# A windowed attention with a two-layer network behind it: early transposes on TensorE, a shorter weight conversion with a second reading, other due times

## The chip, the cores and the metric

The kernel runs on one NeuronCore of one Trainium2 chip. TensorE (PE) multiplies matrices into PSUM, which has eight banks; VectorE (DVE), ScalarE (ACT) and GpSimd (POOL) work on tiles of 128 partitions; SyncE (SP) issues nearly all DMAs, in program order. Each engine works through its own list of instructions in order and waits at semaphores. The metric is the device time of one execution in microseconds, the median of three runs.

## The reference

Attention with a local window and a few global columns, for 4 batches and 8 heads of 768 rows and 64 columns; then a layer of 512 to 2048, a sigmoid gate, and 2048 to 512, on all 3072 rows:

```python
scores = scale * np.matmul(q, k.transpose(0, 1, 3, 2)) + bias      # scale = 1 / sqrt(64)
scores = np.where(is_global | is_local, scores, -1e9)              # n_global = 8, n_local = 96
a = np.exp(scores - np.max(scores, axis=-1, keepdims=True))
a = a / (np.sum(a, axis=-1, keepdims=True) + 1e-09)
x = np.matmul(a, v)            # to (3072, 512)
h = x @ w_in                   # w_in (512, 2048)
g = h * (1.0 / (1.0 + np.exp(-1.702 * h)))
out = g @ w_out                # w_out (2048, 512)
```

q, k and v are float32, the weights float64 (read as pairs of 32-bit words).

## The kernel before

**Attention.** The 3072 rows are 24 blocks of 128 (`n` 0 to 23), six to a batch. A block's rows look at their own block, the one before, and the batch's first 32 columns, so a unit (two of the eight heads, `u` 0 to 3) has score tiles of 128 or 256 columns. `prep` loads a block's q, k and v (three DMAs of 256 KB), splits them into a high and a low float16 (L338 to L348), transposes both by DMA into `QK` (L341) and copies its halves across (the swap, L343). A `unit` is then a chain: scores on TensorE (L377) into the single PSUM buffer `s`; on VectorE mask and row minimum (L383, tile `p` and `NM`); the exponential on ScalarE (L392); a float16 copy (L396) and the remainder (L398) into `hl`; a DMA transpose of both into `pt` (L399); values on TensorE (L408 to L410) into `pv`. `leading` copies the batch's first columns and rows over the block's own when the block is done with its own (L427; L429 is a DMA, `VR<-VG`, that waits for the last values of the block). `finish` divides by the row sum, splits, and transposes by DMA into `xT` (L456).

**Network.** Two blocks make a chunk `c` (0 to 11). The 2048 inner columns are eight slices `s`. `up` multiplies (24 matmuls, L473, tile `h`), then the gate runs: tanh on ScalarE (L482), VectorE (L483), ScalarE (L484), VectorE (L485, tile `g`). `down` adds into `y` (12 matmuls, L500). After slice 7 `y` is scaled and written out (L511, L513). Every product is three float16 products (high by high, high by low, low by high).

**Weights.** For each slice the up half (`u` = 0) and the down half (`u` = 1) are loaded as 1 MiB of word pairs (`ws`, L159). Four passes move the float64's exponent and mantissa into float32 `wa` and two split it into `w`, high and low (L287 to L296). They stay in SBUF. Later ScalarE sums their squares once (L558), for a check; blocks 0 to 3 are loaded once more for theirs (tile `again`). If a check fails, `general` computes everything anew in a slower way; its instructions stand behind a branch.

**What sets the order.** Every step is a task with the engines it may run on, a cost in us, its buffers and a due time. Due times are pulled back from a task's followers, and `order` then plays the queues: on a free engine the ready task with the earliest due time is taken, if its buffers are free and it is due within `AHEAD` = 25 us. The instructions of each engine stand in the order that comes out. Slices of chunks 0 and 1 take turns while weights arrive (`seq`, `PACE0`), later chunks follow one by one (`PACE`). In the tables and rows a tile's name carries block and unit, chunk and slice, or slice and half: `pt2_3` is block 2, unit 3; `h1_0` chunk 1, slice 0; `w3_1` slice 3, down half.

## Time and profile before

| | us |
|---|---|
| median of three runs (lowest to highest) | 664.21 (663.39 to 668.5) |
| the profiled execution, its time | 665.1 |
| its span, first to last instruction | 663.3 |
| TensorE busy | 588.8 |
| ScalarE busy | 427.4 |
| VectorE busy | 412.4 |
| GpSimd busy | 11.6 |

The mean granted clock of TensorE is 0.985. The profile cuts the span into 40 slices of 16.6 us; a digit is the busy share of a slice in tenths:

```profile
PE   0134959999899999999999999999999999999995
DVE  5788789888656557556555655665656645554321
ACT  3677879987557567646656758888755666552321
```

A row of a table of groups reads: line, engine, operation, output <- input, shapes, count | busy us, mean ns of one | idle us of the engine just ahead of them <- what ended it. In rows of stretches each engine's busy us and number of instructions follow the length; PEclk is the granted clock, then the DMA engines' mean busy share (transfers overlap, so it may pass 1) and GB/s. In lists of waits stand total us, times and the longest.

### The profile page before, as it was taken

To read this page: it belongs to the slowest core of one execution; us is meant where nothing else is said; L and a number is where in the kernel's file an instruction comes from. 1 tells how busy PE (TensorE), PEld (TensorE's weight loads), DVE (VectorE), ACT (ScalarE), POOL (GpSimd) and SP (SyncE) were. 2 spreads that over 40 slices of the span, in tenths; PEclk is the share of its full clock that TensorE was granted. 3 is DMA by queue.
4 is the path that set the end of the run, shared out by engine and by line. 5 is a ranking of instruction groups with operands and counts; after the bars stand their busy time and mean duration, and the time that the engine had idled before them with its cause. 6 is when DMAs were issued, how large, how long until landed. Compare 5 with 4: busy or idle time off the path is not lost.

```text
span 663.3 us, 13356 instructions
## 1 busy us (share of the span) xinstructions
PE 588.8 (89%) x5218; PEld 418.1 (63%) x5218; DVE 412.4 (62%) x969; ACT 427.4 (64%) x925; POOL 11.6 (2%) x14
## 2 busy tenths in 40 slices
PE   0134959999899999999999999999999999999995
PEld 0123737677477777677666677776676776776762
DVE  5788789888656557556555655665656645554321
ACT  3677879987557567646656758888755666552321
POOL 1500000000000000000000000000000000000000
PEclk9999989999899999999999999999999999999998
DMA  9999999746968569649619838659819684432001
GB/s 192 243 206 255 243 276 313 205 86 137 227 136 151 125 113 177 136 87 175 152 37 164 158 76 173 137 106 184 186 38 165 143 179 101 95 63 54 33 1 38
DMA packets 270824, 95.61 MB, mean 144 GB/s; under 512 B 257824, under 2 KB 257824, under 8 KB 270752
## 3 DMA queue, kind: packets, MB, share of 16 engines
q1 hardware_dynamic: 270464, 94.66, 67.4%
q8 instruction: 43, 0.70, 0.5%
q14 instruction: 29, 0.24, 0.1%
q10 hardware_dynamic: 288, 0.00, 0.0%
HBM read 38.80 MB, written 6.29 MB: 68 GB/s over the span
## 4 chain that ended last, share of the span: by engine, by line
PE 84%; DMA 7%; DVE 4%; issue 2%; SPq 1%; ACT 1%; DVEq 0%; ACTq 0%
PE h L473 38%; PE y L500 36%; PE s L377 6%; PE pv L408 2%; PE pv L410 2%; PE pv L409 1%; DMA ws<-in_moe_w_in_dram 1%; DMA pt<-hl 1%; DMA QK<-qk 1%; DVE p L383 1%; DMA QK<-QK 1%; DMA VR<-VG 1%; DMA raw<-in_k_dram 1%; DVE qk L339 1%; SPq L341 1%
## 5 line engine op out<-in xcount | busy, mean ns | idle before, releaser
L473 PE MATMUL h<-xT,w 128*128 128x256 f16 x2304 | 269.0, 275 | 3.7 <-DMA xT<-x 3.4
L500 PE MATMUL y<-w,g 128*128 128x512 f16 x1152 | 264.9, 381 | 0.0
L473 PEld LDWEIGHTS <-w 128*128 128x128 f16 x2304 | 223.7, 99 | 33.3 <-issue 4.1
L500 PEld LDWEIGHTS <-g 128*128 128x128 f16 x1152 | 110.1, 98 | 116.8 <-issue 1.9
L392 ACT ACTIVATE p<-p,NM 128x256 f32<-128x256 f32 (+1 forms) x192 | 92.2, 481 | 40.1 <-DVE NM L383 39.4
L482 ACT ACTIVATE t<-h 128x512 f32<-128x512 f32 x96 | 57.0, 593 | 80.5 <-PE h L473 80.0
L383 DVE CUSTOM_DVE_ANT_0 p<-s,mm 128x256 f32<-128x256 f32 (+1 forms) x192 | 69.7, 398 | 61.9 <-PE s L377 61.6
L483 DVE SCALAR_TENSOR_TENSOR t<-t,h 128x512 f32<-128x512 f32 x96 | 65.6, 683 | 61.2 <-ACT t L482 61.1
L377 PE MATMUL s<-QK 128*128 128x128 f16 x384 | 51.4, 234 | 42.4 <-DMA QK<-QK 18.4
L377 PEld LDWEIGHTS <-QK 128*128 128x128 f16 x704 | 48.9, 104 | 63.4 <-DMA QK<-QK 19.1
L485 DVE SCALAR_TENSOR_TENSOR g<-t,g 128x512 f16<-128x512 f32 x96 | 66.1, 688 | 29.4 <-ACT g L484 29.2
L484 ACT ACTIVATE g<-t 128x512 f16<-128x512 f32 x96 | 60.0, 625 | 29.3 <-DVE t L483 28.4
L398 DVE TENSOR_TENSOR hl<-p,hl 128x512 f16<-128x512 f32 (+1 forms) x96 | 61.4, 643 | 23.8 <-ACT hl L396 23.6
L396 ACT CAST hl<-p 128x512 f16<-128x512 f32 (+1 forms) x96 | 55.7, 581 | 6.3 <-DMA pt<-hl 3.8
L408 PE MATMUL pv<-VR,pt 128*128 128x64 f16 x352 | 42.1, 198 | 12.6 <-DMA pt<-hl 8.6
L377 PE MATMUL s<-QK,QK 128*128 128x128 f16 x320 | 43.2, 231 | 7.8 <-DVE NM L383 7.8
L408 PEld LDWEIGHTS <-pt 128*128 128x128 f16 x352 | 33.9, 101 | 18.8 <-DMA pt<-hl 9.6
L410 PE MATMUL pv<-VR,pt 128*128 128x64 f16 x352 | 42.2, 198 | 0.0
L409 PE MATMUL pv<-VR,pt 128*128 128x64 f16 x352 | 42.2, 198 | 0.0
L409 PEld LDWEIGHTS <-pt 128*128 128x128 f16 x352 | 33.1, 101 | 4.5
L392 ACT ACTIVATION_READ_ACCUMULATOR p<-p,NM 128x1 f32 x192 | 36.0, 187 | 0.0
L339 DVE SCALAR_TENSOR_TENSOR qk<-raw,qk 128x1024 f16<-128x1024 f32 x24 | 29.6, 1234 | 9.6 <-ACT qk L338 9.4
(80 smaller groups left out, 392.2 us busy)
## 6 DMA issues: line engine op xcount, KB each, us to landing
ws<-in_moe_w_in_dram SPq DMA_DIRECT2D x8, 1024.0 KB, 6.3
ws<-in_moe_w_out_dram SPq DMA_DIRECT2D x8, 1024.0 KB, 7.6
raw<-in_q_dram SPq DMA_DIRECT2D x24, 256.0 KB, 3.4
raw<-in_k_dram SPq DMA_DIRECT2D x24, 256.0 KB, 3.8
raw<-in_v_dram SPq DMA_DIRECT2D x24, 256.0 KB, 3.6
QK<-QK SPq DMA_DIRECT2D x48, 128.0 KB, 3.4
out_dram<-yo SPq DMA_DIRECT2D x24, 256.0 KB, 2.5
pt<-hl SPq DMA_TRANSPOSE x96, 3.3
```

The costliest lines, as they stand in the source:

```text
L377: nc.tensor.matmul(sp()[:, j, s * P:(s + 1) * P], d["QK"]()[:, 0, h, :], K[:, 1 + z, h, :], start=(z == 0), stop=(z == 1), skip_group_chec ...
L383: nc.vector.tensor_tensor_reduce(out=pr()[:, j, :], in0=sp()[:, j, :], in1=m, scale=-1.0 / SC, scalar=3.0e38, op0=ALU.add, op1=ALU.min, ac ...
L392: ex.append(add({"ACT": 0.48 + 0.1 * ns}, lambda e, j=j: nc.scalar.activation(pr()[:, j, :], pr()[:, j, :], AF.Exp, bias=NM[:, n, hs[j]:hs ...
L398: lambda e: ENG[e].tensor_sub(hl()[:, 1], pr(), hl()[:, 0]), [t4], [pr, hl])
L408: nc.tensor.matmul(o, ph, V[:, 0, h], start=(s == 0), stop=False, skip_group_check=True)
L409: nc.tensor.matmul(o, ph, V[:, 1, h], start=False, stop=False, skip_group_check=True)
L473: nc.tensor.matmul(ph()[:, fi, :], w1(s, cc, z, fi), X[:, y, cc, :], start=(j + cc == 0), stop=(j == 2 and cc == NCC - 1))
L482: t2 = add({"ACT": 0.62}, lambda e: nc.scalar.activation(t(), hh(), AF.Tanh, scale=0.851 / (SX * SW)), [t1], [ph, t])
L483: t3 = add({"DVE": 0.7}, lambda e: nc.vector.scalar_tensor_tensor(t(), t(), 1.0, hh(), ALU.add, ALU.mult), [t2], [ph, t])
L484: t4 = add({"ACT": 0.62}, lambda e: nc.scalar.mul(g()[:, 0], t(), SG / (SX * SW)), [t3], [t, g])
L485: t5 = add({"DVE": 0.7}, lambda e: nc.vector.scalar_tensor_tensor(g()[:, 1], t(), SG / (SX * SW), g()[:, 0], ALU.mult, ALU.subtract), [t4] ...
L500: nc.tensor.matmul(y()[:, t], G[:, zg, fi, t * P:(t + 1) * P], w2(s, z, fi), start=(s == 0 and j == 0 and fi == 0), stop=(s == NST - 1 and ...
```

## The change

Four parts.

1. For blocks 0 to 3 (`EARLY`) TensorE transposes the exponentials themselves, in float32 against an identity matrix, into a PSUM tile `tp`; ScalarE casts them from there into the high half of `pt` and VectorE writes the remainder. `hl` and the DMA transpose drop out for these blocks: 8 transposes for block 0 and 16 each for blocks 1 to 3. The PSUM tiles are borrowed from `y`, which becomes four rings of one bank.
2. In the weights' conversion ScalarE writes the sign as bfloat16 1 or -1 into the upper half of each word of the addend, in place of VectorE's sign mask, and the pass that scaled the exponent (L287) drops out; VectorE shifts `ws` directly. The last two steps now also scale.
3. That holds only for weights in a range of exponents, so all weights are loaded a second time: ScalarE sums the squares of the high words, VectorE takes their minimum, and the end tests both.
4. Due times: attention of chunk 2 and later 60 in place of 46 us ahead of its chunk, `PACE0` 8.0 and `PACE` 5.9, and the checks start from fixed earliest times. Rings: `hl` 3 to 2, `pt` 5 to 4.

```diff
-        t1 = add({"ACT": 1.05}, lambda e: nc.scalar.mul(wa(), ws()[:, :, 1].bitcast(F32), 2.0 ** -111), [t0], [ws, wa])
-        t2 = add({"DVE": 0.7}, lambda e: nc.vector.tensor_scalar(ai(), ai(), 3, None, ALU.logical_shift_left), [t1], [wa])
-        t3 = add({"DVE": 0.75}, lambda e: nc.vector.tensor_scalar(
-            part(1), ws().bitcast(U16)[:, :, 3::4].rearrange("p c o -> p (c o)"), 1 << 15, None, ALU.bitwise_and), [t0], [ws, w])
-        t4 = add({"ACT": 1.05}, lambda e: nc.scalar.mul(part(0), ws()[:, :, 0].bitcast(U32), 2.0 ** -29), [t0], [ws, w])
+        t2 = add({"DVE": 0.75}, lambda e: nc.vector.tensor_scalar(ai(), ws()[:, :, 1], 3, None, ALU.logical_shift_left),
+                 [t0], [ws, wa])
+        t3 = add({"ACT": 1.35}, lambda e: nc.scalar.activation(part(1).bitcast(BF16), ws()[:, :, 1].bitcast(F32), AF.Sign), [t0], [ws, w])
+        t4 = add({"ACT": 1.35}, lambda e: nc.scalar.mul(part(0), ws()[:, :, 0].bitcast(U32), 2.0 ** -29), [t0], [ws, w])
         t5 = add({"DVE": 1.25}, lambda e: nc.vector.tensor_add(ai(), ai(), extra()), [t2, t3, t4], [w, wa])
-        t6 = add({"ACT": 1.05}, lambda e: nc.scalar.copy(w()[:, 0], wa()), [t5], [wa, w])
-        t7 = add({"DVE": 1.25}, lambda e: nc.vector.tensor_sub(w()[:, 1], wa(), w()[:, 0]), [t6], [wa, w])
+        t6 = add({"ACT": 1.05}, lambda e: nc.scalar.mul(w()[:, 0], wa(), 2.0 * SW), [t5], [wa, w])
+        t7 = add({"DVE": 1.25}, lambda e: nc.vector.scalar_tensor_tensor(
+            w()[:, 1], wa(), 2.0 * SW, w()[:, 0], ALU.mult, ALU.subtract), [t6], [wa, w])
...
+        if n < EARLY:
+            tp = Buf(r_y[1, u % 2] if n > 1 else r_y[u // 2, u % 2], [P, 2 * ns, P], F32, f"tp{n}_{u}")
+            def turn(e):
+                for j in range(2):
+                    for s in range(ns):
+                        nc.tensor.transpose(tp()[:, j * ns + s, :], pr()[:, j, s * P:(s + 1) * P], ident)
+            t4 = add({"PE": 2 * ns * 0.215}, turn, ex, [pr, tp])
+            t5 = add({"ACT": 0.2 + 0.21 * ns}, lambda e: nc.scalar.copy(pt()[:, 0:2 * ns], tp()), [t4], [tp, pt])
+            t6 = add({"DVE": 0.15 + 0.27 * ns}, lambda e: nc.vector.tensor_sub(pt()[:, 2 * ns:4 * ns], tp(), pt()[:, 0:2 * ns]),
+                     [t5], [tp, pt])
+        else:
...
-    T0, PACE0, PACE = 25.0, 6.5, 6.05
+    T0, PACE0, PACE = 25.0, 8.0, 5.9
...
-                ws_ = start[c, 0] - 46.0 + 5.2 * ((n % 2) * NU + u)
+                ws_ = start[c, 0] - 60.0 + 5.2 * ((n % 2) * NU + u)
...
+            ws = Buf(r_ws, [P, 1024, 2], I32, f"ws{s}_{u}again")
+            t0 = add({"SP": 3.2}, lambda e, s=s, u=u, ws=ws: load_weights(nc, ws(), w_in, w_out, s, u), bufs=[ws])
+            soon, hi_w = 190.0 + 20.0 * (2 * s + u), lambda ws=ws: ws()[:, :, 1].bitcast(F32)
+            t1 = add({"ACT": 1.35}, lambda e, s=s, u=u, hi_w=hi_w: nc.scalar.activation(
+                hi_w(), hi_w(), AF.Square, accum_out=e2[:, 0, 2 * s + u:2 * s + u + 1]), [t0], [ws])
+            add({"DVE": 1.3}, lambda e, s=s, u=u, hi_w=hi_w: nc.vector.tensor_reduce(
+                e2[:, 1, 2 * s + u:2 * s + u + 1], hi_w(), axis=AX.X, op=ALU.min), [t1], [ws])
+            t0.soon = soon
```

How the order moves, at three places. First SP's queue from the transpose that completes `xT0` on. Before:

```order
L456 DMA_TRANSPOSE xT0_464<-x161_535 128x8x128
L159 DMA ws3_0_558<-in_moe_w_in_dram 128x4x512
L399 DMA_TRANSPOSE pt2_3_617<-hl2_3_556 128x8x128
L159 DMA ws3_1_634<-in_moe_w_out_dram 128x2x1024
L399 DMA_TRANSPOSE pt3_0_707<-hl3_0_615 128x8x128
L399 DMA_TRANSPOSE pt3_1_717<-hl3_1_666 128x8x128
L159 DMA ws4_0_736<-in_moe_w_in_dram 128x4x512
L429 DMA VR2_318<-VG0_238 32x1024
L399 DMA_TRANSPOSE pt3_2_781<-hl3_2_763 128x8x128
L456 DMA_TRANSPOSE xT1_800<-x162_775 128x8x128
L399 DMA_TRANSPOSE pt3_3_808<-hl3_3_779 128x8x128
L159 DMA ws4_1_813<-in_moe_w_out_dram 128x2x1024
```

The same stretch after the change, up to the transpose that completes `xT1`:

```order
L476 DMA_TRANSPOSE xT0_366<-x161_517 128x8x128
L449 DMA VR2_176<-VG0_161 32x1024
L319 DMA raw4_497<-in_v_dram 128x8x64
L164 DMA ws3_0_766<-in_moe_w_in_dram 128x4x512
L164 DMA ws3_1_788<-in_moe_w_out_dram 128x2x1024
L476 DMA_TRANSPOSE xT1_857<-x162_784 128x8x128
L319 DMA raw5_864<-in_q_dram 128x8x64
L319 DMA raw5_864<-in_k_dram 128x8x64
L449 DMA VR3_309<-VG0_161 32x1024
L164 DMA ws4_0_920<-in_moe_w_in_dram 128x4x512
L476 DMA_TRANSPOSE xT1_857<-x163_918 128x8x128
```

The transposes of `pt` are gone, and the copy into `VR2`, which stood behind the weights of slice 4, now stands ahead of those of slice 3.

Second, ScalarE between the first gate's end and the third, where the down half of slice 2 gets its cast. Before:

```order
L484 ACTIVATE g0_0_769<-t0_0_709 128x512
L482 ACTIVATE t0_1_771<-h0_1_682 128x512
L293 ACTIVATE w3_0_720<-ws3_0_558 128x1024
L396 CAST hl3_3_779<-p3_3_711 128x512
L293 ACTIVATE w3_1_784<-ws3_1_634 128x1024
L482 ACTIVATE t0_2_803<-h0_2_738 128x512
L484 ACTIVATE g0_1_806<-t0_1_771 128x512
L295 CAST w3_0_720<-wa3_0_714 128x1024
L293 ACTIVATE w4_0_840<-ws4_0_736 128x1024
L295 CAST w2_1_541<-wa2_1_621 128x1024
L484 ACTIVATE g0_2_857<-t0_2_803 128x512
```

After, from the second gate's tanh on:

```order
L504 ACTIVATE g0_1_862<-t0_1_794 128x512
L301 ACTIVATE w2_1_809<-ws2_1_394 128x1024
L502 ACTIVATE t0_2_894<-h0_2_829 128x512
L300 ACTIVATE w3_0_912<-ws3_0_766 128x1024
L301 ACTIVATE w3_0_912<-ws3_0_766 128x1024
L300 ACTIVATE w3_1_924<-ws3_1_788 128x1024
L301 ACTIVATE w3_1_924<-ws3_1_788 128x1024
L303 ACTIVATE w2_1_809<-wa2_1_915 128x1024
L504 ACTIVATE g0_2_935<-t0_2_894 128x512
```

The cast of `w2_1` stood behind conversions of slices 3 and 4; it now stands behind the sign and the low word (L300, L301) of both halves of slice 3.

Third, TensorE at the start of batch 1's attention (block 6). Before:

```order
L377 MATMUL s6_0_1900<-QK6_1801 128x128
L377 LDWEIGHTS QK6_1801
L377 MATMUL s6_0_1900<-QK6_1801 128x128
L377 LDWEIGHTS QK6_1801
L377 MATMUL s6_1_1916<-QK6_1801 128x128
L377 LDWEIGHTS QK6_1801
L377 MATMUL s6_1_1916<-QK6_1801 128x128
```

After:

```order
L385 MATMUL s6_0_1894<-QK6_1764 128x128
L385 LDWEIGHTS QK6_1764
L385 MATMUL s6_0_1894<-QK6_1764 128x128
L520 LDWEIGHTS g1_6_1846
L520 MATMUL y1_0_1071<-w6_1_1252,g1_6_1846 128x512
L520 LDWEIGHTS g1_6_1846
L520 MATMUL y1_0_1071<-w6_1_1252,g1_6_1846 128x512
```

Unit 1's scores directly followed unit 0's; now a whole down of chunk 1 stands between them. The same holds for the other blocks.

More of the change, by code (lines that the diff above doesn't have):

```diff
@@ L26 @@
 LOW = 1e8
+EARLY = 4
 AHEAD = 25.0
@@ L61, in __init__, with early @@
         self.on, self.fn, self.after, self.bufs, self.due = on, fn, list(after), list(bufs), want
-        self.next, self.end, self.eng, self.start = [], None, None, None
+        self.next, self.end, self.eng, self.start, self.soon = [], None, None, None, 0.0
+    def early(self):
+        return self.soon if self.due > 1e8 else self.due - AHEAD
 class Work:
@@ L107, in order @@
                 for t, at in ready.items():
-                    if e not in t.on or at > now or t.due > now + AHEAD or (best is not None and t.due >= best.due):
+                    if e not in t.on or at > now or t.early() > now or (best is not None and t.due >= best.due):
                         continue
@@ L146, in order @@
             if not moved:
-                later = [t.due - AHEAD + 1e-6 for t in ready if t.due > now + AHEAD]
+                later = [x + 1e-6 for x in (t.early() for t in ready) if x > now]
                 later += [x for x in (*free.values(), dma - BACKLOG + 1e-6) if x > now] + [at for at in ready.values() if at > now]
@@ L216 @@
     nc.vector.tensor_add(odd, odd, o2)
+    ident = const.tile([P, P], F32, name="ident")
+    make_identity(nc, ident)
     mm = const.tile([P, H, 3, P], BF16, name="mm")
@@ L252 @@
     swt = const.tile([P, 2, NST], F32, name="swt")
+    e2 = const.tile([P, 2, 2 * NST], F32, name="e2")
     junk = const.tile([P, 1024], BF16, name="junk")
@@ L265 @@
     r_s, r_pv = ring("s", 1, ps), ring("pv", 1, ps)
-    r_h, r_y = ring("h", 2, ps), ring("y", 2, ps)
+    r_h = ring("h", 2, ps)
+    r_y = {(z, t): ring(f"y{z}{t}", 1, ps) for z in range(2) for t in range(2)}
     r_w = {(s, u): ring(f"w{s}_{u}", 1) for s in range(NST) for u in range(2)}
@@ L490, in down @@
         if s == 0:
-            ys[c] = Buf(r_y, [P, 2, DM], F32, f"y{c}")
+            ys[c] = [Buf(r_y[c % 2, t], [P, DM], F32, f"y{c}_{t}") for t in range(2)]
         y = ys[c]
@@ L510, in down @@
                 t2 = add({"DVE": 0.7, "ACT": 0.65}, lambda e, t=t, yo=yo: (
[L511 to L512 removed]
+                    nc.vector.tensor_scalar(yo(), y[t](), f, None, ALU.mult) if e == "DVE" else nc.scalar.mul(yo(), y[t](), f)),
+                    [t1], [y[t], yo], want + 4)
                 add({"SP": 0.7}, lambda e, t=t, yo=yo: nc.sync.dma_start(
@@ L554 @@
         raw = Buf(r_raw, [P, 3, H, D], F32, f"again{n}")
-        guard(n, raw, load(n, raw), t_ - 150.0 + 20 * n)
+        ld = load(n, raw)
+        guard(n, raw, ld, 1e9)
+        for t in ld:
+            t.soon = 400.0 + 30 * n
     for s in range(NST):
```

28 lines of the change are left out of this document (14 added, 14 removed).

## The prediction

> **What bounds the kernel now.** I read the busy shares first, then one table of stages cut where the chain of waits turns.
>
> ```profile
> PE 588.8 (89%) x5218; PEld 418.1 (63%) x5218; DVE 412.4 (62%) x969; ACT 427.4 (64%) x925; POOL 11.6 (2%) x14
> ```
>
> ```profile
> core 0: us, PE busy (x) PEld busy (x) DVE busy (x) ACT busy (x) POOL busy (x), PEclk, DMA share, GB/s
> 0.00:33.00 33.00, 3.02 (x19) 1.92 (x19) 21.21 (x64) 16.15 (x31) 11.62 (x14) 1.00 0.97 217
> 33.00:66.00 33.00, 12.67 (x138) 10.40 (x139) 27.62 (x66) 25.39 (x54) 0.00 (x0) 1.00 1.17 230
> 66.00:98.10 32.10, 23.81 (x233) 16.84 (x232) 26.31 (x53) 25.21 (x43) 0.00 (x0) 0.94 1.10 256
> 98.10:178.30 80.20, 77.30 (x644) 54.13 (x644) 68.95 (x133) 65.97 (x126) 0.00 (x0) 0.97 0.76 197
> 178.30:655.20 476.90, 471.86 (x4188) 334.77 (x4186) 266.84 (x647) 294.08 (x675) 0.00 (x0) 0.99 0.59 118
> 655.20:663.30 8.10, 0.17 (x3) 0.06 (x2) 1.48 (x9) 0.60 (x1) 0.00 (x0) 0.65 0.21 76
> ```
>
> There are two regimes. From 98.1 us to 655.2 TensorE is the bound: it works 549.2 of 557.1 us. Before 98.1 it works only 39.5 us, while the DMA share stands at or above 1: there the transfers are the bound. The chain of waits says what they hold up, and the list of PE's waits after 100 us what is left later:
>
> ```profile
> 71.01 2.62 PE h L473 x24
> ...
> 80.54 5.59 DMA VR<-VG
> ...
> 94.70 3.40 DMA xT<-x
> ...
> 98.14 9.55 PE h L473 x72
> ...
> 655.25 0.14 PE pb L583 x2
> ```
>
> ```profile
> PE s L377 <- DVE NM L383: 7.6, 7, 1.7
> PE h L473 <- DVE t L483: 0.2, 1, 0.2
> ```
>
> So the time is the start T of h1_0 (chunk 1's first up-projection, 98.14 now), plus 557.1 us of nearly gapless TensorE, plus a tail of 8.05 us. In both orders the same TensorE work stands ahead of h1_0: attention of blocks 0 to 3, three ups, three downs. That makes T a fair mark.
>
> **Step 1, transposes off the DMA queue.** Sixteen transposes (blocks 0 to 3) leave SP's queue.
>
> ```profile
> L399 SPq DMA_TRANSPOSE pt<-hl x16: 1214/1376/4092, 30.2 to 85.8; - x16
> ...
> DMA to landing us min/median/max: 2.5/5.8/9.9
> ```
>
> I count bytes from the rows of the order and the tiles' shapes. Up to the transpose that completes xT0 (it frees h0_0) the old queue moves 14.75 MiB: 3 of raw, 6 of weights, 2 of QK, 1 of swaps, 2.25 of pt, 0.5 of xT. The new one moves 13.0: no pt, but 0.5 of raw4 pulled forward. With the transfers as the bound, h0_0 comes at 71.01 x 13.0 / 14.75 = 62.6. Up to the transpose that completes xT1 it is 21.5 against 17.25 MiB, so transfers alone would allow T = 98.14 x 17.25 / 21.5 = 78.7. That is the lower end.
>
> **The wait that takes its place.** The new queue puts VR2<-VG0 (the copy of the leading rows into block 2's values) ahead of raw4's v, both halves of weights 3, both transposes of xT1 and weights 4_0. The copy waits for the last values matmul of block 2, which TensorE's order now puts behind h0_0 and h0_1. That this copy waits for TensorE is old:
>
> ```profile
> SPq L429 <- PE pv L410: 32.1, 6, 9.3
> ```
>
> From h0_0 at 62.6 to that matmul TensorE has two ups, two score units, two groups of four transposes and three of values. Its clock decides how long:
>
> ```profile
> 38.28 0.42 PE L377 MATMUL s<-QK 128*128 128x128 f16 x2
> 38.49 0.42 PE L377 MATMUL s<-QK,QK 128*128 128x128 f16 x2
> ...
> 86.97 4.44 PE L500 MATMUL y<-w,g 128*128 128x512 f16 x12
> ...
> 91.95 2.75 PE L500 MATMUL y<-w,g 128*128 128x512 f16 x12
> ```
>
> Two 128-column matmuls start 0.21 us before the next two, 0.107 each: half speed, since the dense stretch does twelve of 512 columns in 2.75 us and the one after the wait at 80.54 needed 4.44. I take the first up at about 4.3 (2.62 x 4.44 / 2.75), the second at 2.6, and 4.3 for the small groups: 11.2, so the copy is issued near 73.8. Then 4.25 MiB (4.46 MB) follow; at the 256 GB/s of the 66 to 98.1 row that is 17.4 us, and some 2 us until the first lands: xT1 is whole near 93.2. ScalarE gives the same time: it takes the third down's weight cast (w2_1) only behind both halves of weights 3, which land near 85; two conversions, the cast, g's two steps and the down end near 93. **T = 93**, 5.1 earlier. Between the ends 78.7 and 98.1 I take a value near the upper one because of this wait, and because of ScalarE's share: it has done 66.8 us by 98.1, 78% of the time from 33 on. Counted by the order with the durations of the rows, the new one leaves it 2.2 less by h1_0's tanh; T = 93 asks for 77%, T = 78.7 for 100%, T = 86 for 87%.
>
> **What TensorE gets.** 56 f32 transposes of 128 columns; none is in the trace. Lower end 0.107 each (6 us), upper four such passes (24 us). Most run before 62, in the 58.6 idle us ahead of 98.1; 20 run behind h0_0 and lie in the 4.3 and in T. I take 0.2. The Trainium skill, "TensorE: Matmul & The Clock Gate", section on the PE-mode transpose, gives about 275 ns in a kernel, by which the 56 would be 15.4 us, and says that transposes do not count as activity for the clock; no trace here shows it. The eviction's two steps keep their sizes (casts and subtractions of the same shapes):
>
> ```profile
> L396 ACT CAST hl<-p 128x512 f16<-128x512 f32 x80 | 49.2, 617 | 5.6 <-DMA pt<-hl 3.5
> L398 DVE TENSOR_TENSOR hl<-p,hl 128x512 f16<-128x512 f32 x80 | 54.8, 687 | 23.0 <-ACT hl L396 22.9
> ```
>
> **Step 2, the weights' exponents.** A tile costs ScalarE 1.144 + 1.354 + 1.040 and VectorE 0.765 + 0.686 + 1.228 + 1.234 now.
>
> ```profile
> L293 ACT ACTIVATE w<-ws 128x1024 uint16<-128x1024 uint32 x16 | 21.7, 1354 | 2.4 <-DMA ws<-in_moe_w_out_dram 2.4
> L296 DVE TENSOR_TENSOR w<-wa,w 128x1024 f16<-128x1024 f32 x16 | 19.6, 1234 | 0.3 <-ACT w L295 0.3
> L294 DVE CUSTOM_DVE_ANT_0 wa<-wa,w 128x2048 uint16<-128x2048 uint16 x16 | 19.5, 1228 | 1.2 <-ACT w L293 0.8 <-issue 0.2
> L287 ACT ACTIVATE wa<-ws 128x1024 f32<-128x1024 f32 x16 | 18.2, 1144 | 13.1 <-DMA ws<-in_moe_w_in_dram 7.6 <-DMA ws<-in_moe_w_out_dram 5.5
> L295 ACT CAST w<-wa 128x1024 f16<-128x1024 f32 x16 | 16.5, 1040 | 2.3 <-DVE wa L294 2.3
> L291 DVE TENSOR_SCALAR w<-ws 128x1024 uint16<-128x1024 uint16 x16 | 12.2, 765 | 6.0 <-DMA ws<-in_moe_w_out_dram 3.1 <-DMA ws<-in_moe_w_in_dram 2.9
> L288 DVE TENSOR_SCALAR wa<-wa 128x1024 int32<-128x1024 int32 x16 | 10.9, 686 | 1.3 <-ACT wa L287 1.2
> ```
>
> Afterwards the sign (written every second 16-bit word, as L293 does) costs 1.144 to 1.354, I take the latter: ScalarE +0.21, +3.4 in all. VectorE loses one pass, about -0.70 a tile, -11.2 in all. A tile's first VectorE step no longer waits for ScalarE. This lies in the early stage, inside T; it earns nothing by itself where the queue is late.
>
> **Step 3, the second reading.** 16 MiB more, 16.8 MB. At the rate of a stretch full of weights it takes 53.6 us of the queue, spread between about 190 and 500 us, where the DMA share of 0.59 has room (16.8 MB over 477 us raises it by about 0.11). ScalarE gets 16 squares with a sum (1.144 + 0.19), VectorE 16 minima:
>
> ```profile
> 99.50:116.10 16.60, 16.60 (x123) 12.17 (x122) 15.98 (x22) 15.80 (x23) 0.00 (x0) 0.95 1.04 313
> ```
>
> ```profile
> L318 ACT ACTIVATION_READ_ACCUMULATOR junk<-raw 128x1 f32 x40 | 7.6, 190 | 0.0
> L569 DVE TENSOR_REDUCE fin<-NM 128x1 f32<-128x192 f32 x1 | 0.3, 346 | 0.0
> ```
>
> The minimum, 1024 elements, lies between 0.346 and 5.3 times that; I take about 1.2. ScalarE +21, VectorE +19 beside 294 and 267 of 477: covered, as long as no square holds up an exp behind it while its load is still on the way. I allow 3 us for such waits, from 0 to rival 3's price.
>
> **Step 4, attention sooner.** All seven of PE's late waits are at places where two score units stand directly behind each other; the single `s` buffer makes the second wait for VectorE. In the new order something else of TensorE's stands between any two units from block 0's third on. That removes the 7.8 us of the two rows. What is late next: nothing in the row, TensorE itself. Around the first such place it also loses its clock:
>
> ```profile
> 174.00:181.00 7.00, 4.14 (x28) 2.99 (x26) 3.65 (x20) 6.89 (x24) 0.00 (x0) 0.67 1.03 243
> ```
>
> 0.33 of 7 us, 2.3 us, goes with the waits. At nothing I cost the separate y banks and the shorter rings (hl 3 to 2, pt 5 to 4), since the list of late waits names neither y nor pt and the units now come 14 us sooner; the identity matrix on POOL, which works 11.6 of the first 33 us; four small VectorE steps more ahead of the last sum, done under TensorE's last three downs; and block 0's scores, which come some us earlier (their swap now precedes weights 0_1) but are followed by block 1's, whose swap still stands behind weights 1_0.
>
> **Sum.** 93 + (557.1 - 7.8 - 2.3 + 3) + 8.05 = 651.05. The profiled run took 665.1 for a span of 663.3 (+1.8) and lies 0.9 over the median of 664.21, so 652.
>
> **Rivals.** 1. The earlier start is given back: ScalarE (65.97 of 80.2 us between 98.1 and 178.3) cannot take the later half of the weights faster, h2_0 starts at 178.3 as now, and only the 5.0 idle us behind it go: 658.3, as a time 659. For it: VectorE and ScalarE at 82% or more there; against: VectorE loses 11 us. 2. The queue does not wait so long (h0_0 warm, the copy early), T = 86, with 0 to 3 us of new waits: 642 to 645. For it: transfers alone allow 78.7. 3. Slower: the squares wait for their loads.
>
> ```profile
> ws<-in_moe_w_out_dram SPq DMA_DIRECT2D x8, 1024.0 KB, 7.6
> ```
>
> ScalarE keeps its order, so a square ahead of its data holds exps, tanhs and at last TensorE. At 2 us each, 652 - 3 + 32 = 681; it decides from 1.4 us each (671), and 7.6 would be the whole landing. Against it: they are issued in a stage with slack. 4. The clock stays at half through blocks 2 and 3, because transposes do not wake it: three ups and three downs of 2.6 at nearly double, some 11 us on T after the queue's cover: 663, no change. Against it: h0_0 alone is 24 ordinary matmuls, and now the clock rises within the first such groups. The rule of the Trainium skill's "TensorE: Matmul & The Clock Gate" named above would lead here. 5. The new check refuses these weights, and the general path recomputes everything: more than double the time.
>
> **Chances.** Forecast (T 89 to 97; 648 to 657) 0.56; rival 1 0.19; rival 2 0.14; rival 3 0.06; rival 4 0.04; rival 5 0.01. A measurement here tells about 1%, 657.6 to 670.9 being no change. Faster: 0.56 + 0.14 = 0.70; same: 0.19 + 0.04 = 0.23; slower 0.07. The range takes in most of rivals 1 and 2: 642 to 661.
>
> **What would show it.** h0_0 near 63; VR2<-VG0 issued near 74 with SP waiting on values matmuls and the DMA share dipping under 1 ahead of it; h1_0 near 93; no wait of PE on NM after 100; ScalarE waiting little on the second weights. It is wrong if h1_0 starts before 86 or after 98, if PE idles over 8 us between h1_0 and the end, or if transposes take over 0.43 us each.

## The result and the profile after

The changed kernel takes 646.18 us (median of four runs, 644.56 to 647.04) against 666.36 us for the kernel before in the same session (663.39 to 670.38): a ratio of 0.969, 95% interval 0.963 to 0.975. It is faster, by 20 us; the prediction said 652. The profiled execution took 644.56 us, the shortest of the four, for a span of 642.8.

First the busy shares and the table of stages, cut at the same events as before (the fourth row starts shortly ahead of chunk 1's first up, the fifth at chunk 2's first up, the last behind the last down). Columns as in the prediction: each engine's busy us with its instructions, the granted clock, DMA share, GB/s.

```profile
PE 590.3 (92%) x5274; PEld 419.9 (65%) x5274; DVE 420.5 (65%) x980; ACT 439.8 (68%) x950; POOL 11.9 (2%) x16
```

```profile
core 0: us, PE busy (x) PEld busy (x) DVE busy (x) ACT busy (x) POOL busy (x), PEclk, DMA share, GB/s
0.00:33.00 33.00, 6.50 (x45) 4.46 (x45) 19.08 (x63) 16.81 (x32) 11.94 (x16) 1.00 0.96 213
33.00:59.90 26.90, 14.64 (x164) 11.79 (x165) 21.48 (x59) 21.36 (x50) 0.00 (x0) 0.96 1.04 252
59.90:87.00 27.10, 23.18 (x232) 16.66 (x232) 25.06 (x50) 22.90 (x39) 0.00 (x0) 0.88 0.66 164
87.00:166.00 79.00, 77.13 (x647) 53.49 (x646) 65.97 (x122) 70.86 (x128) 0.00 (x0) 0.99 0.81 203
166.00:634.70 468.70, 468.70 (x4191) 333.47 (x4188) 287.34 (x680) 307.66 (x704) 0.00 (x0) 1.00 0.73 157
634.70:642.80 8.10, 0.15 (x3) 0.04 (x2) 1.54 (x9) 0.23 (x1) 0.00 (x0) 0.71 0.22 76
```

Three things to see. Behind 166 us TensorE has no gap left, 468.70 of 468.70, where it had 5 us of gaps. In the third row the DMA share has fallen to 0.66, from 1.10 in the stretch ahead of h1_0 before: the transfers are no longer what bounds the early stage. And there VectorE works 25.06 of 27.10 us: something else has come close.

The timeline gives the marks. SyncE's queue first (start us, us of issuing, what):

```profile
56.61 1.31 SPq L476 DMA_TRANSPOSE xT<-x  x1
68.81 0.55 SPq L449 DMA_DIRECT2D VR<-VG  x1
...
70.09 1.58 SPq L164 DMA_DIRECT2D ws<-in_moe_w_in_dram  x1
...
80.95 1.45 SPq L476 DMA_TRANSPOSE xT<-x  x1
```

Then TensorE's; in brackets how long it waited ahead of the row, and for what:

```profile
59.85 3.47 PE L493 MATMUL h<-xT,w 128*128 128x256 f16 x24 [0.15 <-DMA xT<-x]
...
83.69 5.18 PE L520 MATMUL y<-w,g 128*128 128x512 f16 x12 [3.92 <-ACT g L504]
89.13 5.41 PE L493 MATMUL h<-xT,w 128*128 128x256 f16 x48 [0.26 <-DMA xT<-x]
```

SyncE stands from 57.9 to 68.8 before the copy into VR2, as forecast, and xT1 is whole 8 us after its last transpose was issued. Chunk 1's first up, h1_0, starts at 89.13 in place of 98.14. It waited 0.26 us for xT1, and the third down ahead of it 3.92 for a gate of ScalarE, after which its twelve matmuls took 5.18 us, nearly double (the granted clock is 0.50 from 81.8 to 88.6).

Below, T is the start of h1_0 and "rest" the time from T to TensorE's last sum (655.18 before, 634.66 after). Then follow 8.1 us of tail. So the 20.5 us of span come from T (98.14 to 89.13, 9.0) and from the rest (557.0 to 545.5, 11.5).

### The profile page after: what moved, and what is told of

The parts are those of the page before. It is cut to its first block, busy times and chain, and to the rows that moved or that the text cites. A ratio compares the mean times of both kernels' runs of the same rounds, so it can differ in the third digit from the quotient of the medians.

```text
span 642.8 us, 13486 instructions
## 1 busy us (share of the span) xinstructions
PE 590.3 (92%) x5274; PEld 419.9 (65%) x5274; DVE 420.5 (65%) x980; ACT 439.8 (68%) x950; POOL 11.9 (2%) x16
## 4 chain that ended last, share of the span: by engine, by line
PE 85%; DMA 6%; DVE 3%; POOL 1%; SPq 1%; ACT 1%; issue 1%; DVEq 0%; ACTq 0%
PE h L493 38%; PE y L520 37%; PE s L385 5%; DMA ws<-in_moe_w_in_dram 2%; PE pv L428 1%; PE pv L430 1%; PE pv L429 1%; POOL mm L256 1%; DMA QK<-qk 1%; DMA QK<-QK 1%; SPq L319 1%; DMA raw<-in_k_dram 1%; DMA raw<-in_v_dram 1%; DVE p L391 1%; DMA xT<-x 0%
## 5 line engine op out<-in xcount | busy, mean ns | idle before, releaser
L391 DVE CUSTOM_DVE_ANT_0 p<-s,mm 128x256 f32<-128x256 f32 (+1 forms) x192 | 70.0, 399 | 65.1 <-PE s L385 63.4
L504 ACT ACTIVATE g<-t 128x512 f16<-128x512 f32 x96 | 59.9, 624 | 24.8 <-DVE t L503 24.1
L385 PE MATMUL s<-QK 128*128 128x128 f16 x384 | 49.0, 227 | 30.3 <-DMA QK<-qk 17.3
L385 PEld LDWEIGHTS <-QK 128*128 128x128 f16 x704 | 46.5, 101 | 43.9 <-DMA QK<-qk 17.3
L418 DVE TENSOR_TENSOR hl<-p,hl 128x512 f16<-128x512 f32 (+1 forms) x80 | 51.8, 648 | 19.2 <-ACT hl L417 18.9
L417 ACT CAST hl<-p 128x512 f16<-128x512 f32 (+1 forms) x80 | 46.8, 585 | 2.3
L385 PE MATMUL s<-QK,QK 128*128 128x128 f16 x320 | 41.6, 225 | 3.3 <-DVE NM L391 3.2
L430 PE MATMUL pv<-VR,pt 128*128 128x64 f16 x352 | 40.9, 194 | 2.2 <-DVE pt L413 2.0
L428 PE MATMUL pv<-VR,pt 128*128 128x64 f16 x352 | 41.3, 194 | 1.7 <-DMA VR<-VG 1.6
L429 PE MATMUL pv<-VR,pt 128*128 128x64 f16 x352 | 41.3, 194 | 0.0
L428 PEld LDWEIGHTS <-pt 128*128 128x128 f16 x352 | 32.9, 99 | 5.2 <-DMA VR<-VG 0.3
L429 PEld LDWEIGHTS <-pt 128*128 128x128 f16 x352 | 32.1, 99 | 6.3 <-issue 1.8
L430 PEld LDWEIGHTS <-pt 128*128 128x128 f16 x352 | 32.0, 99 | 2.7 <-DVE pt L413 2.7
```

Source lines behind the costliest of these rows:

```text
L385: nc.tensor.matmul(sp()[:, j, s * P:(s + 1) * P], d["QK"]()[:, 0, h, :], K[:, 1 + z, h, :], start=(z == 0), stop=(z == 1), skip_group_chec ...
L391: nc.vector.tensor_tensor_reduce(out=pr()[:, j, :], in0=sp()[:, j, :], in1=m, scale=-1.0 / SC, scalar=3.0e38, op0=ALU.add, op1=ALU.min, ac ...
L428: nc.tensor.matmul(o, ph, V[:, 0, h], start=(s == 0), stop=False, skip_group_check=True)
L429: nc.tensor.matmul(o, ph, V[:, 1, h], start=False, stop=False, skip_group_check=True)
L430: nc.tensor.matmul(o, pl, V[:, 0, h], start=False, stop=(s == ns - 1), skip_group_check=True)
L504: t4 = add({"ACT": 0.62}, lambda e: nc.scalar.mul(g()[:, 0], t(), SG / (SX * SW)), [t3], [t, g])
```

## The experiments

Each run was compared with the kernel before on the same chip. T and rest are read from its profile; MB is the GB/s of the stretch from 0 to T, times T.

| run | time, us | ratio to before, 95% interval | T | rest | MB ahead of T |
|---|---|---|---|---|---|
| before | 666.36 | | 98.14 | 557.0 | 23.0 |
| after | 646.18 | 0.969 (0.963 to 0.975) | 89.13 | 545.5 | 18.7 |
| e1, no transposes on TensorE | 672.67 | 1.010 (1.005 to 1.015) | 115.06 | 547.5 | 28.1 |
| e6, in two blocks only | 653.93 | 0.980 (0.977 to 0.984) | 94.93 | 548.7 | 23.1 |
| e5, before with the new due times | 657.13 | 0.987 (0.984 to 0.990) | 95.22 | 550.7 | 22.4 |
| e12, e5 with the shorter rings | 672.72 | 1.008 (1.005 to 1.010) | 117.55 | 547.2 | 28.1 |
| e3, after with the old due times | 652.03 | 0.981 (0.974 to 0.988) | 88.37 | 553.3 | 19.8 |
| e2, no second reading | 647.1 | 0.972 (0.968 to 0.976) | 91.69 | 545.5 | 18.8 |
| e7, old weights' steps | 648.48 | 0.974 (0.970 to 0.978) | 89.79 | 548.9 | 19.5 |
| e4, the copies on GpSimd's queue | 663.85 | 0.996 (0.992 to 0.999) | 84.37* | 569.3 | |
| e8, only the early ones | 651.24 | 0.976 (0.972 to 0.980) | 95.17 | 546.7 | 19.5 |
| e9, weights 3 ahead of the copy | 643.57 | 0.964 (0.961 to 0.966) | 87.03 | 544.3 | 19.5 |
| e10, w2_1's cast sooner | 646.46 | 0.967 (0.963 to 0.971) | 90.29 | 545.8 | 18.7 |
| e11, both | 645.98 | 0.967 (0.965 to 0.970) | 87.90 | 547.2 | 18.5 |

\* In e4 h1_0 stands ahead of the third down, so that its rest holds one down more.

T is that of one execution of each kernel. The order of e2 up to h1_0 is the changed kernel's, and yet its T is 2.6 us later. The granted clock is the likely reason: in the changed kernel it falls to a half from 57.9 to 61.3, just as h0_0 starts; in e2 it does so from 51.5 to 54.9 and from 58.4 to 65.1. The changed kernel first, then e2:

```profile
57.90:61.30 3.40, 3.25 (x23) 2.58 (x21) 2.11 (x7) 2.42 (x5) 0.00 (x0) 0.50 0.41 82
```

```profile
51.50:54.90 3.40, 3.40 (x39) 3.31 (x40) 3.15 (x12) 3.17 (x9) 0.00 (x0) 0.50 1.08 373
58.40:65.10 6.70, 5.62 (x40) 4.62 (x40) 4.77 (x14) 4.20 (x12) 0.00 (x0) 0.50 0.36 78
```

So differences in T of up to some 3 us prove nothing by themselves; where experiments lie closer than that, the waits have to be read.

### e1: all transposes by DMA

```diff
-EARLY = 4
+EARLY = 0
```

> All blocks' exponentials go by DMA transpose again (EARLY = 0), the rest as changed; the order puts 26.25 MiB ahead of h1_0 in place of 17.25. Theory A (transfers set the early stage): h1_0 starts at 100 to 118, well behind 89.1, no late waits of PE on NM come back, TensorE from h1_0 to the end takes at most the 545.6 us of the changed kernel (more weights are already there), time 655 to 672. Theory B (the vector and scalar work sets it, the transposes were only hidden work): h1_0 within 3 us of 89.1, time 644 to 649.

It took 672.67 us, T 115.06, where TensorE waited 15.21 us for xT1. The rest, 547.5, is as good as the changed kernel's, so the whole loss is T. T lies in the range expected of the transfers, the time just above it. But it also shows something not asked for: with the transposes back on the queue the kernel is slower than the one before, which had them there too. e5 and e12 take that up.

### e6: transposes on TensorE in blocks 0 and 1 only

```diff
-EARLY = 4
+EARLY = 2
```

> Only blocks 0 and 1 go over TensorE (EARLY = 2). The order puts 21.5 MiB ahead of h1_0, as many as before the change, against 17.25 with four blocks and 26.25 with none. Theory A (h1_0 follows the bytes ahead of it): h1_0 at 96 to 101, nothing else lost, time 653 to 659. Theory B (half the transposes, half the gain over the kernel with none, by VectorE's and ScalarE's chain and not by bytes): h1_0 between 89 and 95, time 645 to 652.

653.93 us, T 94.93 after a wait of 6.65 us for xT1: half the blocks give back 5.8 us of T. T lies in theory B's range and the time in theory A's, so the numbers alone do not choose; the wait and the stretch from 0 to T do. That stretch in e1, e6 and after:

```profile
0.00:115.06 115.06, 40.64 (x388) 29.32 (x389) 87.93 (x191) 86.07 (x146) 11.27 (x16) 0.93 1.09 244
```

```profile
0.00:94.93 94.93, 44.55 (x412) 31.53 (x413) 73.66 (x177) 70.01 (x128) 11.69 (x16) 0.89 1.04 243
```

```profile
0.00:89.13 89.13, 46.19 (x444) 33.36 (x445) 67.45 (x172) 62.12 (x121) 11.94 (x16) 0.94 0.89 210
```

In e1 and e6 the share stands above 1 and the rate is the same, 244 and 243 GB/s, while the orders put 26.25 and 21.5 MiB ahead of h1_0 (28.1 and 23.1 MB by the traces): T goes with the bytes, as in theory A. In the changed kernel 18.7 MB would at that rate be done at 77, which is close to the lower end of the forecast (78.7), but the share is 0.89: it no longer follows the bytes.

### e5 and e12: due times and rings on the kernel before

e5 takes the kernel before with the new due times:

```diff
-    T0, PACE0, PACE = 25.0, 6.5, 6.05
+    T0, PACE0, PACE = 25.0, 8.0, 5.9
...
-                ws_ = start[c, 0] - 46.0 + 5.2 * ((n % 2) * NU + u)
+                ws_ = start[c, 0] - 60.0 + 5.2 * ((n % 2) * NU + u)
```

e12 adds the shorter rings:

```diff
-    r_pr, r_hl, r_pt = ring("pr", 3), ring("hl", 3), ring("pt", 5)
+    r_pr, r_hl, r_pt = ring("pr", 3), ring("hl", 2), ring("pt", 4)
```

> The kernel before with the new due times alone (60 us ahead, paces 8.0 and 5.9). The order has no pair of score units behind each other after h1_0, and 21.0 MiB ahead of it in place of 21.5. Theory A (the pairs' waits and the lost clock at block 6 are what the due times are worth, and h1_0 stays a matter of the transfers): no wait of PE on NM after 100 us, TensorE from h1_0 to the end 545 to 548 us in place of 557.1, h1_0 at 96 to 100, time 654 to 659. Theory B (the due times only help together with the early start): 662 to 668.

> The kernel before with two parts of the change: the new due times, and the shorter rings (2 buffers for the halves of the exponentials, 4 for the turned ones). Transposes by DMA for all blocks, the old weights' steps, no second reading. By its order 26.25 MiB stand ahead of the first up of chunk 1, as in the run with all transposes by DMA (e1), against 21.0 with the new due times alone (e5). Theory A (the shorter rings make the attention units wait for one another, and the loads of the weights are put ahead of them, which is why e1 was slower than the kernel before): first up of chunk 1 at 111 to 118, time 667 to 676 us, with e1. Rival (e1's loss is of the second reading, the new weights' steps or the split accumulators): first up of chunk 1 at 95 to 103 and a time of 654 to 660 us, as in e5.

The due times alone bring 1.3% (interval 1.0 to 1.6), some 9 us: the rest falls from 557.0 to 550.7, T by 2.9. The time is in theory A's range, but T is just below its 96 to 100, and the rest above its 545 to 548, with new waits for `xT`, for weights and for `pt` (3.8 us in all behind 100) where those on NM went. The shorter rings then take the ratio from 0.987 to 1.008, some 14 us. In the profiles T is 22.3 us later and the rest 3.5 shorter:

```profile
0.00:95.22 95.22, 41.84 (x389) 30.62 (x389) 72.91 (x177) 65.11 (x124) 11.62 (x14) 1.00 1.06 235
```

```profile
0.00:117.55 117.55, 42.15 (x388) 30.05 (x389) 91.96 (x201) 83.05 (x144) 11.60 (x14) 0.95 1.08 239
```

The same TensorE work, 389 and 388 matmuls, has 22.4 MB ahead of it in the one and 28.1 in the other. The list of TensorE's waits in e12 up to 130 us (total, times, longest) names the place:

```profile
PE pv L408 <- DMA pt<-hl: 17.7, 9, 8.4
```

In e5 this wait is 6.1 us at four places in the whole run. The order puts 26.25 MiB ahead of h1_0 in e12 and 21.0 in e5, so with the shorter rings the planner sets more loads ahead of xT1; that it does so because the units wait for a free buffer is the likely course, and which of the two rings does it was not separated. e12 agrees with e1 in time and bytes, within 2.5 us in T, and in this wait (17.7 us at nine places in e1 too), so e1's loss against the kernel before is that of the rings, not of the second reading or of the weights. It fits that the changed kernel can have the short rings because its first four blocks use no `hl`. But the changed kernel without early transposes and with the long rings was not tried, so e1 overstates what these transposes are worth: from e5 to the changed kernel T falls by 6.1 us and the rest by 5.2, and in that the transposes, the new weights' steps and the rings may all have a part.

### e3: the old due times in the changed kernel

```diff
-    T0, PACE0, PACE = 25.0, 8.0, 5.9
+    T0, PACE0, PACE = 25.0, 6.5, 6.05
...
-                ws_ = start[c, 0] - 60.0 + 5.2 * ((n % 2) * NU + u)
+                ws_ = start[c, 0] - 46.0 + 5.2 * ((n % 2) * NU + u)
```

> Only the due times are the old ones again (46 us ahead, paces 6.5 and 6.05). The order then has six pairs of score units directly behind each other after h1_0, at blocks 6, 12, 18 and 22, as against none in the changed kernel and seven before. Theory A (each such pair costs TensorE a wait for VectorE, 0.6 to 1.7 us, and at block 6 its full clock): 4 to 9 us of waits on NM after h1_0 return, time 650 to 656. Theory B (the waits are hidden in slack elsewhere or go with the y banks): no waits on NM, time 644 to 648. h1_0 stays near 89 in both, since the early order changes little (18.25 MiB ahead of it in place of 17.25).

652.03 us, theory A: T stays (88.37), the rest grows from 545.5 to 553.3. The list of TensorE's waits behind 100 us, of e3 and then of the changed kernel:

```profile
PE s L385 <- DVE NM L391: 5.3, 6, 1.2
PE h L493 <- DVE t L503: 1.9, 2, 1.1
```

```profile
PE s L385 <- DVE NM L391: 0.5, 1, 0.5
```

The waits of one score unit for the other's row minimum come back with the old due times and go with the new ones, in both kernels (e5: also 0.5 in one).

### e2: without the second reading

The second loads, their squares and minima are left out, and at the end the lines with `eok` that test them.

```diff
-            t0 = add({"SP": 3.2}, lambda e, s=s, u=u, ws=ws: load_weights(nc, ws(), w_in, w_out, s, u), bufs=[ws])
...
-            t1 = add({"ACT": 1.35}, lambda e, s=s, u=u, hi_w=hi_w: nc.scalar.activation(
-                hi_w(), hi_w(), AF.Square, accum_out=e2[:, 0, 2 * s + u:2 * s + u + 1]), [t0], [ws])
-            add({"DVE": 1.3}, lambda e, s=s, u=u, hi_w=hi_w: nc.vector.tensor_reduce(
-                e2[:, 1, 2 * s + u:2 * s + u + 1], hi_w(), axis=AX.X, op=ALU.min), [t1], [ws])
```

> The second reading of the weights and its test are left out (16 MiB of loads, 16 squares, 16 minima); the order of the early stage is the same. Theory A (it is wholly covered, TensorE being the bound after 166): time within 1 us of the changed kernel's, 645 to 647. Theory B (squares and minima cost TensorE some waits): 1 to 5 us faster, 641 to 645. The trace of the changed kernel shows no idle TensorE after 166, so A is expected.

647.1 us, not to be told from 646.18, and the same rest, 545.5 (theory A). 16 MiB of transfers, 16 squares and 16 minima cost nothing that can be measured here. The changed kernel's list of ScalarE's waits from 190 us on:

```profile
ACT ws_0again L587 <- DMA ws_0again<-in_moe_w_in_dram: 2.8, 2, 2.6
ACT ws_1again L587 <- DMA ws_1again<-in_moe_w_out_dram: 2.7, 4, 1.2
```

Six of the 16 squares waited for their load, 5.5 us in all, and TensorE has no gap at any of them.

### e7: the old steps of the weights' conversion

```diff
-        t2 = add({"DVE": 0.75}, lambda e: nc.vector.tensor_scalar(ai(), ws()[:, :, 1], 3, None, ALU.logical_shift_left),
-                 [t0], [ws, wa])
-        t3 = add({"ACT": 1.35}, lambda e: nc.scalar.activation(part(1).bitcast(BF16), ws()[:, :, 1].bitcast(F32), AF.Sign), [t0], [ws, w])
+        t1 = add({"ACT": 1.05}, lambda e: nc.scalar.mul(wa(), ws()[:, :, 1].bitcast(F32), 2.0 ** -111), [t0], [ws, wa])
+        t2 = add({"DVE": 0.7}, lambda e: nc.vector.tensor_scalar(ai(), ai(), 3, None, ALU.logical_shift_left), [t1], [wa])
+        t3 = add({"DVE": 0.75}, lambda e: nc.vector.tensor_scalar(
+            part(1), ws().bitcast(U16)[:, :, 3::4].rearrange("p c o -> p (c o)"), 1 << 15, None, ALU.bitwise_and), [t0], [ws, w])
```

with the two last steps unscaled again, and the planner's cost of the low word back at 1.05.

> The weights are converted by the old steps (the scaled pass and VectorE's sign mask), the second reading and all else as changed; VectorE works 11 us more in the first 160. The order has one pair of score units after h1_0 (block 6) and 18.25 MiB ahead of h1_0. Theory A (the shorter conversion lies beside the transfers and the wait of the queue, worth little): h1_0 at 88 to 93, one wait of 1 to 2 us, time 645 to 650. Theory B (VectorE, 92% busy between 59.9 and 87, sets the early stage): h1_0 at 94 or later, or idle TensorE while the weights come, time 651 to 658.

648.48 us, T 89.79, rest 548.9. The intervals of the two ratios overlap, so the 2.3 us are at the edge of what can be told (theory A). Part of the 3.4 us of rest is not the conversion itself: the other order brings back one pair of score units at block 6, and the waits on NM behind T are 1.8 us in place of 0.5. The conversion is worth some 2 us, not more.

### e4 and e8: the copies into VR on GpSimd's queue

SyncE's wait before the copy into VR2 was the prediction's reason for T = 93. Both runs take it off SyncE, e4 (the diff) for all blocks, e8 for blocks 1 to 3 alone, with a cost of 4.0.

```diff
-        d["VG"].append(add({"SP": 0.3}, lambda e: nc.sync.dma_start(d["VR"]()[0:NG], VG()), [*d["V"], blk["VGr", b]],
+        d["VG"].append(add({"POOL": 2.5}, lambda e: nc.gpsimd.dma_start(d["VR"]()[0:NG], VG()), [*d["V"], blk["VGr", b]],
```

> The copies VR<-VG go out on GpSimd's queue in place of SyncE's, the rest as changed, so that SyncE no longer stands still from 58 to 68.8 us behind the last values of block 2. Theory A (that wait sets T): the loads of slice 3 start 8 to 10 us sooner, the wait of the third down (3.9 us) and the one for weights 4_0 go, h1_0 starts at 81 to 86, time 637 to 643. Theory B (ScalarE's conversions set T, or the early gain is given back to ScalarE between h1_0 and the end of the weights): time 644 to 648, with h1_0 at 86 or later or with new TensorE idle behind it.

> The copies VR<-VG go out on GpSimd's queue for blocks 1 to 3 alone; later ones stay on SyncE. Theory A (in the run with all of them on GpSimd the early start was won, h1_0 at 84.4, and lost again where TensorE waited 12.3 us for late copies and then ran at half its clock): h1_0 at 83 to 87, TensorE 545 to 548 us from there, time 638 to 643. Theory B (something else of that kernel cost the time, the work of ScalarE and VectorE between h1_0 and 166): h1_0 at 83 to 87 but TensorE takes 550 us or more, time 644 to 652.

e4: h1_0 comes at 84.37, as hoped, and the time is still 663.85. e8: h1_0 at 95.17 and 651.24. e4's time is outside both theories; e8's is in the range of its theory B, but by another way: h1_0 is 8 us later than either theory had it, and the rest is 546.7, where B had 550 or more. In e4 the list of TensorE's waits shows where it went, and the list of DMA issues (count, KB, median us to landing) why:

```profile
PE pv L428 <- DMA VR<-VG: 11.9, 6, 3.2
```

```profile
VR<-VG POOLq DMA_DIRECT2D x16, 64.0 KB, 3.2
```

The copy lands 3.2 us after GpSimd issues it, against 2.0 from SyncE's queue in the changed kernel, and the next block's values wait for it at six places; around them the clock falls as well (the stretch 166 to 300 has a granted clock of 0.97 and 9 us of gaps, where the changed kernel has none). In e8 one copy took 6.90 us in the chain of waits, block 3's values and chunk 0's third up stood behind it, and the planner, told another cost, put the queue in another order. Both runs changed the order at many places, so they say little on what set T.

### e9, e10, e11: the two chains ahead of h1_0, by hand

Three runs therefore keep the planner's order and move single steps in it. `put(a, b)` takes step a out and sets it ahead of step b; `tag[s, u]` holds a weight tile's steps (0 the load, 2 the shift L298, 3 the sign L300, 4 the low word L301, 5 the sum L302, 6 the cast L303, 7 the remainder L304), `tag["g", 0, 2]` the last two steps of the third gate, `tag["x", 3]` the cast ahead of xT1's last transpose. e9:

```diff
+        put(tag[1, 1][4], tag[1, 1][3])
+        put(tag[1, 1][3], tag[1, 1][4])
+        put(tag[3, 0][0], tag["VR", 2])
+        put(tag[3, 1][0], tag["VR", 2])
```

e10, and e11 has the lines of both:

```diff
+        put(tag[2, 1][5], tag["x", 3])
+        put(tag[2, 1][6], tag[3, 1][3])
+        put(tag["g", 0, 2][0], tag[3, 1][3])
+        put(tag[2, 1][7], tag[3, 0][2])
+        put(tag["g", 0, 2][1], tag[3, 0][2])
```

> The changed kernel with its order altered by hand at one place: both loads of weights 3 (2 MiB) go to SyncE ahead of the copy of block 2's global values (the one before which SyncE stood from 57.9 to 68.8 us), and the sign step of w1_1 goes to ScalarE right behind that tile's first step, so that the buffer for weights 3 is free some 8 us sooner. Theory A (two chains end together at the first up of chunk 1: the queue behind SyncE's wait, and the third down behind the cast of w2_1 on ScalarE): the second half of xT1 lands 3 to 5 us sooner, but the third down still ends near 88.9, so the first up of chunk 1 stays at 87.5 to 89.5 and the time at 644 to 648 us. Theory B (SyncE's wait alone sets it): the first up of chunk 1 at 83 to 86, time 639 to 643 us. Theory C (ScalarE is so full there that one step put ahead delays block 3's attention by as much): first up of chunk 1 at 89.5 to 92, time 647 to 650 us.

> The changed kernel with its order altered by hand at the other place only: the sum, cast and remainder of w2_1 and the gate of the third down go ahead of the steps of w3_1 on ScalarE and of w3_0's on VectorE; the two instructions that prepare the second half of x for xT1 stand 1.2 us later on VectorE for it. SyncE's order is as in the changed kernel. Theory A (two chains): the third down starts near 81.5 and ends near 85 in place of 88.9, but the second half of xT1 lands at 89 to 91, so TensorE now waits 4 to 6 us for it and the first up of chunk 1 stands at 89 to 91.5, time 645 to 649 us. Theory B (SyncE's wait alone sets it): the same first up, but then also e9 gains. Theory C (ScalarE alone sets it): first up of chunk 1 at 84 to 86.5, time 640 to 643 us.

> Both alterations of the order together: weights 3 ahead of the copy of block 2's global values, and w2_1 with the third down's gate ahead of the rest of weights 3. Theory A (two chains that end together): only here does the first up of chunk 1 move, to 84 to 86.5, and the time to 640 to 644 us, a gain that neither of the two has alone. If one chain alone sets it, this run is like the one of the two that gains, within 1 us. If a third thing sets it (the values of block 3, late on ScalarE), the first up stays at 88 to 90 and the time at 644 to 648 us.

The first two lines of e9 bring the low word of w1_1 right behind its sign (60.45 us in place of 68.36), which frees the buffer for weights 3. e9, SyncE's timeline and TensorE's:

```profile
59.49 0.39 SPq L164 DMA_DIRECT2D ws<-in_moe_w_in_dram  x1
61.82 0.37 SPq L164 DMA_DIRECT2D ws<-in_moe_w_out_dram  x1
68.02 0.55 SPq L449 DMA_DIRECT2D VR<-VG  x1
...
79.02 1.27 SPq L476 DMA_TRANSPOSE xT<-x  x1
```

```profile
82.89 4.30 PE L520 MATMUL y<-w,g 128*128 128x512 f16 x12 [3.91 <-ACT g L504]
87.03 8.02 PE L493 MATMUL h<-xT,w 128*128 128x256 f16 x72
```

The 2 MiB of weights 3 now go out under the wait for VR2. h1_0 no longer waits for xT1 at all. Yet T moves by 2.1 us only, since the third down still waits 3.91 us for its gate and runs slow behind that wait. Even of these 2.1 us some 1.6 are the clock: the first up takes 2.78 us in place of 3.47, the third down 4.30 in place of 5.18. By the waits that is theory A. T (87.03) is just ahead of the 87.5 to 89.5 expected there, and the time, 643.57, lies between its 644 to 648 and theory B's 639 to 643. It is the lowest of all runs; against the changed kernel the intervals of the ratios overlap.

e10, TensorE's timeline:

```profile
90.29 9.60 PE L493 MATMUL h<-xT,w 128*128 128x256 f16 x72 [2.72 <-DMA xT<-x]
```

Now the third down ends sooner (87.6), and h1_0 waits 2.72 us for xT1: theory A again, 646.46 us. Whichever of the two is shortened, the other stands right behind it.

e11 has both, and theory A's gain (84 to 86.5) does not come: T 87.90, 645.98 us. T is within 1 us of e9's, which had been named as the sign that one chain alone sets it, and just ahead of the 88 to 90 named for a third thing. The waits speak for the latter. TensorE's timeline:

```profile
83.03 1.04 PE L520 MATMUL y<-w,g 128*128 128x512 f16 x4 [2.59 <-ACT g L504]
84.88 3.18 PE L520 MATMUL y<-w,g 128*128 128x512 f16 x8 [0.82 <-DVE w L304]
87.90 5.40 PE L493 MATMUL h<-xT,w 128*128 128x256 f16 x48
96.04 2.78 PE L493 MATMUL h<-xT,w 128*128 128x256 f16 x24 [2.74 <-DVE t L503]
```

There is no wait for xT1. The third down waits, for ScalarE and then for VectorE's remainder, and the third up from h1_0 on waits 2.74 us for VectorE to free its PSUM buffer. The stage 59.9 to 87 of e11, and of e9:

```profile
59.90:87.00 27.10, 23.45 (x246) 17.12 (x245) 25.15 (x53) 23.82 (x43) 0.00 (x0) 0.95 0.65 176
```

```profile
59.90:87.00 27.10, 23.19 (x236) 16.70 (x235) 25.45 (x49) 25.78 (x42) 0.00 (x0) 0.94 0.72 209
```

VectorE works 93 to 94% of this stage, ScalarE 88 and 95%. With the queue and the cast out of the way, these two engines are likely what is left, and a step put ahead of another on them only moves the wait. e11's profile also ran 1.5 us later than e9's from h0_0 on (61.21 against 59.75); its granted clock is 0.50 from 50.0 to 56.8, e9's from 48.6 to 51.9, so a part of its missing gain can be the clock. So that the queue and ScalarE end together within some 3 us is shown by the waits of e9 and e10; that VectorE is the third is read from e11's waits and shares, and no run took work from it.

## Why the prediction was right, and where it was off

**The model held.** The time is T, a nearly gapless stretch of TensorE, and the tail, in all of the runs: T + rest + 8.1 gives the span of each within 0.4 us. The forecast had T = 93, a rest of 550.0 and 652 us; it came to 89.1, 545.5 and 646.2. T lies at the edge of its own range (89 to 97), the time just under 648 to 657 and inside 642 to 661. The mechanisms were the right ones; several terms were off, nearly all towards a longer time.

**Step 1, the early stage.** That the transfers stop being the bound, and that T nevertheless stays far above the 78.7 which the bytes allow, was right: the DMA share ahead of T is 0.89, and SyncE stood before VR2. The size was off at two terms. h0_0 was put at 62.6 by scaling with the bytes and came at 59.85. And from there to the copy 11.2 us were counted, with the first up at 4.3 and the small groups at half pace, 4.3 more; it took 9.0 (59.85 to 68.81): the first up 3.3, the small groups 2.8, since TensorE was at full pace again by 63. Together the copy was issued 5.0 us sooner than forecast. Much of this is the luck of one execution: in e2, with the same order up to there, h0_0 starts at 61.83, the first up takes 4.3, the copy goes out at 71.72 and T is 91.69. The next term, 19.4 us from the copy to a whole xT1, was nearly right with 20.3. ScalarE's chain, put at 93 too, ended at 88.9. That both chains end together was right (with the queue's taken away in e9 the wait for the gate stays, with ScalarE's shortened in e10 the one for xT1 comes up). Left out was VectorE: the share of ScalarE from 33 us on was weighed, 78%, but by the same two rows VectorE had 53.9 of 65.1 us, 83%; after the change it is 48.4 of 56.1, 86%. Whether it holds T up was not tested.

**Transposes on TensorE.** Taken at 0.2 each between 0.107 and four times that. Rows of four, cold and warm, and the whole group (min, median, max ns):

```profile
42.48 1.06 PE L409 MATMUL tp<-ident,p 128*128 128x128 f32 x4
...
48.15 0.61 PE L409 MATMUL tp<-ident,p 128*128 128x128 f32 x4
```

```profile
L409 PE MATMUL tp<-ident,p x56: 272/278/477, 25.3 to 73.2; 128*128 128x128 f32 x56
```

One of them lasts 0.28 us warm, but four take 0.61: they start 0.11 us apart, and 0.21 at half pace. The lower end was nearly the truth where the clock was up.

**Step 2, the weights.** The sign took 1354 ns as taken, ScalarE's addition is as forecast, and "earns nothing by itself" holds within 2.3 us (e7). **Step 3, the second reading:** covered, and the 3 us allowed for waits were not needed (e2: the same rest to 0.1 us). The square with its sum took 1.33 us and the minimum 1.21, where 1.33 and 1.2 had been taken. **Step 4, the due times:** 7.8 us of waits and 2.3 of clock were to go; this term was too small. In e3 the old due times bring back 7.8 us of rest, in e5 the new ones take 6.3 of it and 2.9 of T, the latter no more than T's spread. From before to after the gaps in the rest fell from 7.9 to 1.6 us and the busy time from 549.2 to 543.9, for the same 4829 matmuls, so more came through the clock (5.2) than the 2.3 read from one place. Before, the clock was at a half in two stretches of the rest, together 9.0 busy us, of which half, 4.5, is lost; after, it is in none:

```profile
98.14:101.30 3.16, 3.16 (x16) 2.16 (x16) 3.16 (x5) 3.13 (x7) 0.00 (x0) 0.50 1.02 379
176.39:183.22 6.83, 5.83 (x31) 4.28 (x31) 4.21 (x17) 5.09 (x18) 0.00 (x0) 0.50 0.87 209
```

The forecast's window ended at 181 and had only the second of them.

**Costed at nothing:** the rings. In the changed kernel no wait of TensorE's on `pt<-hl` is left that they could have caused; on the kernel before the same line costs some 14 us (e12). The sentence gave as its reason that no late wait names `pt`; the likelier one is that the early blocks no longer go through `hl`. In e5, with three buffers, ScalarE's casts into it still waited 4.2 us at five places for a transpose to free one.

**The rivals.** Nothing was given back (rival 1): chunk 2's first up starts at 165.85 in place of 178.36, 12.5 us sooner, more than T's 9.0. Rival 2's T of 86 was not reached, though its "no new waits" was. The squares' waits (rival 3) did not reach TensorE. The clock (rival 4) went the other way.
